# ScalarE's squares, tangents and projection casts: which instruction the weight work is issued behind

## The chip, the cores and the metric

The kernel runs on one core of a Trainium2 chip. The metric is the device time of one execution in microseconds; lower is better. The engines are called by the names the profile gives them: PE (TensorE), ACT (ScalarE), DVE (VectorE), POOL (GpSimd) and SP (SyncE, which only issues transfers here).

## What is computed

A block of 2048 tokens and 512 features goes through a layer norm, then through two branches: attention with 32 heads of 16 features over a sliding window of 256 tokens, and a gated feed-forward of width 1792. The second branch gates the first.

```python
xn = _layernorm(x, axis=-1)
s = _A_ref(xn, A_wqkv, A_wo)              # sliding-window attention
g = _silu(_B_ref(xn, B_w1, B_w3, B_w2))   # (silu(xn @ w1) * (xn @ w3)) @ w2
return x + s * g
```

## The kernel before, in words

All products are made in float16 with a high and a low half of each operand (three matmuls for one product: high by high, high by low, low by high). So each weight is prepared on the chip before its first use, and kept in DRAM for later use. The preparation of a weight tile has these steps, in this order:

- a square with a sum over the row: on ACT (`L249`, tile `sqa`, with the sums `ssq`) or, for some tiles, on DVE; for the down projection's weight w2 it is `L931`
- a cast of the sums to bf16 on DVE (`L261`, or `L935` for w2; tile `sb`)
- a small sum over all rows on PE (`L285`, `s<-sb,onesb`), placed in spare columns of an attention scores bank, beside the matmuls of a maxima row (`L667`)
- a power of two from this sum on DVE (`L294`, `L295`, `L298`, `L302`, `L304`, and for w2 `L946` to `L956`)
- the scaling on ACT (`L342`), the high half on ACT (`L343`), the low half on POOL (`L345`); for some tiles both on ACT and DVE (`L333`, `L334`)

The tokens are done in four tiles of 512 (t = 0 to 3). In each tile, the attention goes over 4 groups of heads (g) and 2 pairs in each (p). A first pass makes the scores on PE (`L667`, tiles `s` and `po`) and their maxima on DVE (`L681`); a second pass makes them again with the maximum in a row of the operand (`L748`), adds a mask on DVE (`L755`), takes the exponential on ACT (`L758`, tile `pt`) and multiplies by the values on PE (`L776`, tile `po`). Beside these batches stand dense pieces: q and k projections (PE `L597`, upper half cast by ACT `L614`, lower half by DVE `L618`), the values (`L567`, `L570`), gate and up products of the feed-forward (PE `L1048`; ACT's tanh of the gate `L1063`, DVE's `L1067`, and `L1072` for the product with up; then the halves by ACT `L1081` and POOL `L339`), and the down products (`L1273`, later `L1191` in a folded form with seven products, whose weights are sums made at t = 1 by ACT `L1003`, POOL `L1005` to `L1019` and ACT `L1015`). In tiles t > 0 the layer norm's scale comes from POOL (`L465` to `L474`, tile `rs`), and DVE applies it (`L477`).

What sets the order: PE's instructions stand in the order in which the program writes them. The other engines' queues are put in order by a scheduler, each engine then working strictly down its list. Two things bind the scheduler. `urgent()` raises the priority of an instruction. `tc.issue_after(ins)` puts what it encloses behind the instruction `ins` in the queue; the helper `behind_exp()` uses the instruction held in `lasts["exp"]`. Before the change that is the last attention exponential. It binds scalings of later gate and up weights (`tied`), squares and scalings of w2, the fold's sums, and the tanh of the output gate. `lasts["emptied"]` holds DVE's last instruction that empties a bank.

`later(n, f)` runs `f` n program steps later. `squares(..., apart=1)`, which `measure(f, 1)` calls for the gate and up weights of two blocks of 128 columns, spreads the four squares of such a pair over four steps. `f` counts these blocks, 14 in all. The squares of the pairs f = 6, 8, 10 and 12 run beside the first attention units.

The names in the code blocks and rows: `slot_N` is the N-th tile made in the general memory of 54 slots, `m` a PSUM bank of a dense piece, `s` and `po` PSUM tiles of the attention. Line numbers are those of the kernel before; in the kernel after, all lines from 253 on are 3 higher.

Of the kernel before, what the change touches and what calls it, by code (L numbers as in the profile page):

```python
# [14 lines left out]
AF = mybir.ActivationFunctionType  # L15
# [68 lines left out]
def tile_block(ctx: ExitStack, tc: tile.TileContext, x, wqkv, wo, w1, w3, w2, out):  # L84
    nc = tc.nc
# [58 lines left out]
    def later(n, f):  # L144
        made_so_far[0] += 1
        queue.append((now[0] + n, made_so_far[0], f))
# [33 lines left out]
    behind = []  # L180
# [59 lines left out]
    def squares(parts, on_act=0, apart=0):  # L240


        ssq = small.tile([P, len(parts)], F32, name="ssq")

        def one(i, raw):

            sq = ppool.tile([P, D], BF16, name="sqa" if i < on_act else "junk", bufs=1)
            if i < on_act:
                nc.scalar.activation(sq, raw, AF.Square, accum_out=ssq[:, i:i + 1])  # L249
            else:  # L250
                nc.vector.tensor_tensor_reduce(out=sq, in0=raw, in1=raw, scale=1.0, scalar=0.0,
                                               op0=ALU.mult, op1=ALU.add, accum_out=ssq[:, i:i + 1])
        for i, raw in enumerate(parts):
            if apart:
                later(apart * (i + 1), lambda i=i, raw=raw: one(i, raw))
            else:
                one(i, raw)
        sb = small.tile([P, len(parts)], BF16, name="sb")

        def cast():  # L260
            lasts["cast"] = nc.vector.tensor_copy(sb, ssq)  # L261
        def behind_bank():

            with tc.issue_after(lasts["emptied"].ins) if "emptied" in lasts else nullcontext():
                cast()
        if apart:
            later(apart * len(parts) + 2, behind_bank)
        else:
            cast()
        return sb  # L270
# [151 lines left out]
    lasts = {}  # L422
# [158 lines left out]
    def project(t, g, k, terms=(range(3),), scores_bank=False):  # L581


        cell = {}

        parts = ([[(c, i) for c in (2 * half, 2 * half + 1) for i in range(3)] for half in range(2)] if len(terms) == 1
                 else [[(c, i) for i in group for c in range(NC)] for group in terms])

        def part(n):
            assert turned[t] == 4  # L590
            w = WQ[t, g, k]
            xh, xl = X[t]
            if n == 0:
                cell["pp"] = bank([P, TW]) if scores_bank is False else scores_bank()[:, 0, :]
            for c, i in parts[n]:
                a, b = ((0, xh), (1, xh), (0, xl))[i]
                nc.tensor.matmul(cell["pp"], w[:, (a * NC + c) * P:(a * NC + c + 1) * P], b[:, c, :], start=(c, i) == parts[0][0],  # L597
                                 stop=(c, i) == parts[-1][-1])
            if n < len(parts) - 1:
                return  # L600
            if t == 0:
                def store():
                    with behind_load():
                        nc.sync.dma_start(dWQ[g, k], w)
                    give(w, after=8)
                later(45, store)
            else:
                give(w)
            pp = cell["pp"]
            both = take(F16)  # L610
            B = both.rearrange("p (a t) -> p a t", a=2)
            s = QS / (XS * WS)
            with urgent():
                nc.scalar.activation(B[:, 0, :], pp, AF.Copy, scale=s)  # L614

            def rest():
                with urgent():
                    lasts["emptied"] = nc.vector.scalar_tensor_tensor(B[:, 1, :], pp, s, B[:, 0, :], op0=ALU.mult, op1=ALU.subtract)  # L618
                d = (dQ, dK)[k][g][:, :, t * TW:(t + 1) * TW]
                if k == 0:  # L620
                    nc.sync.dma_start(d[:, 0:2, :], B[:, 0:1, :].to_broadcast([P, 2, TW]))
                    nc.sync.dma_start(d[:, 2, :], B[:, 1, :])
                else:
                    nc.sync.dma_start(d[:, 0:2, :], B)
                    nc.sync.dma_start(d[:, 2, :], B[:, 0, :])
                give(both, after=4)
            later(1, rest)
        return opening([(len(l), lambda n=n: part(n)) for n, l in enumerate(parts)])
# [408 lines left out]
    def gate_up(t, f):  # L1037
        cell = {}

        def part(k, half):  # L1040
            assert turned[t] == 4
            xh, xl = X[t]
            w = WF[t, f][0][k]
            if half == 0:
                cell[k] = bank([P, TW])
            for c in (2 * half, 2 * half + 1):
                for i, (a, b) in enumerate(((0, xh), (1, xh), (0, xl))):
                    nc.tensor.matmul(cell[k], w[:, (a * NC + c) * P:(a * NC + c + 1) * P], b[:, c, :], start=c == 0 and i == 0,  # L1048
                                     stop=c == NC - 1 and i == 2)
            if half == 0:  # L1050
                return
            if t == 0:
                def store():
                    nc.sync.dma_start(dW1[f, k], w)
                    give(w, after=4)
                later(2, store)
            else:
                give(w)
            if k == 0:
                cell["s"] = sg = take(F32)  # L1060

                with urgent():
                    nc.scalar.activation(sg, cell[0], AF.Tanh, scale=sg_scale[:, f:f + 1])  # L1063

                def product():
                    with urgent():
                        lasts["emptied"] = nc.vector.scalar_tensor_tensor(sg, sg, 1.0, cell[0], op0=ALU.add, op1=ALU.mult)  # L1067
                later(1, product)
            else:
                sg = cell["s"]  # L1070
                with urgent():
                    lasts["emptied"] = nc.vector.scalar_tensor_tensor(sg, cell[1], 0.5 * HS / (WS * XS)**2, sg,  # L1072
                                                                      op0=ALU.mult, op1=ALU.mult)
                if t > 1:
                    HH[t, f] = sg
                    later(1, lambda: (fold_second if f % 2 else fold_first)(t, f // 2))
                    return
                HH[t, f] = hh = take(F16)

                def rest():  # L1080
                    nc.scalar.copy(hh[:, 0:TW], sg)  # L1081
                    halves(nc.gpsimd.tensor_sub, hh[:, TW:], sg, hh[:, 0:TW])
                    give(sg, after=8 if t == 0 else 20)
                later(1, rest)
        return [q for k in range(2) for q in opening([(6, lambda k=k, half=half: part(k, half)) for half in range(2)])]
# [604 lines left out]
```

## Time and profile before

| what | value |
|---|---|
| median of 3 runs | 808.35 us (808.19 to 809.09) |
| profiled execution, its own time | 808.19 us |
| its span in the profile | 806.4 us |
| PE busy | 792.3 us (98%) |
| DVE, ACT, POOL busy | 630.9, 392.5, 377.5 us |
| squares on ACT by L249 | 34, median 629 ns, from 6.7 to 146.0 us |
| squares on ACT by L931 | 14, median 621 ns, from 43.8 to 191.4 us |

How to read the views: a timeline row has the start in us, the length in us, the engine, the source line, the operation, output and inputs, the shape, and in brackets how long the engine stood idle before it and what ended that. The name in the bracket is inferred; where the engine named had long been done, it was another. Rows marked x2 and more are merged. A row of the windows view has the window, its length, then busy time and count of PE, of PE's weight loads, of DVE, ACT and POOL, the granted PE clock, the DMA share and GB/s.

### The profile page before, as it was taken

How to read it: one execution, taken by the hardware profiler on the slowest of the kernel's cores; microseconds unless marked ns; L12 is line 12 of the kernel's file. 1: busy time of each engine (PE TensorE's matmuls, PEld its weight loads, DVE VectorE, ACT ScalarE, POOL GpSimd, SP SyncE). 2: the span in 40 equal slices, each digit the busy share in tenths (PEclk: the TensorE clock that was granted, in tenths of full speed). 3: DMA queues.
4: the chain of work that ended last, by engine and by line, in shares of the span. 5: the costliest groups of instructions: out<-in, count | busy, mean ns of one | idle time of the engine just before them, and what ended most of it. 6: DMA issues, size and time to landing. Idle time of an engine off the chain costs nothing.

```text
span 806.4 us, 23975 instructions
## 1 busy us (share of the span) xinstructions
PE 792.3 (98%) x9175; PEld 403.6 (50%) x9175; DVE 630.9 (78%) x2037; ACT 392.5 (49%) x591; POOL 377.5 (47%) x732
## 2 busy tenths in 40 slices
PE   8999999999999999999999999999999999999997
PEld 4444444444544444444445444466544754466465
DVE  8888888798898778887888888777768886875537
ACT  6878686663456535345443443434444234344411
POOL 2345357352439345355352555430346276650670
PEclk9999999999999999999999999999999999999999
DMA  9887554746666574658456733656462654334431
GB/s 282 241 259 241 176 177 121 260 121 196 189 194 197 151 241 129 220 150 268 118 180 177 216 110 94 187 150 186 133 169 84 160 135 132 87 89 158 129 93 59
DMA packets 109859, 134.19 MB, mean 166 GB/s; under 512 B 18928, under 2 KB 64944, under 8 KB 109744
## 3 DMA queue, kind: packets, MB, share of 16 engines
q1 hardware_dynamic: 109456, 132.13, 55.9%
q8 instruction: 72, 1.18, 0.6%
q10 hardware_dynamic: 288, 0.52, 0.2%
q14 instruction: 43, 0.35, 0.1%
HBM read 91.23 MB, written 36.57 MB: 158 GB/s over the span
## 4 chain that ended last, share of the span: by engine, by line
PE 83%; DVE 6%; ACT 6%; DMA 2%; issue 2%; SPq 1%; POOL 0%; DVEq 0%; ACTq 0%
PE m L1048 30%; PE po L776 9%; PE m L1273 9%; PE m L597 8%; PE m L1191 8%; PE s L748 5%; PE m L1325 4%; PE m L567 4%; PE s L667 3%; PE po L667 2%; ACT pt L758 1%; DVE junk L681 1%; ACT slot L342 1%; DMA slot<-in_B_w_dram 1%; ACT slot L343 1%
## 5 line engine op out<-in xcount | busy, mean ns | idle before, releaser
L1048 PE MATMUL m<-XH,slot 128*128 128x512 f16 x896 | 267.3, 380 | 1.3 <-DVE slot L618 0.8
L758 ACT ACTIVATE pt<-s,es 128x1024 f32<-128x1024 f32 x152 | 167.6, 1113 | 190.9 <-DVE s L755 179.2
L1048 PEld LDWEIGHTS <-slot 128*128 128x128 f16 x1344 | 124.9, 98 | 155.2 <-issue 11.5
L1048 PE MATMUL m<-XL,slot 128*128 128x512 f16 x448 | 169.8, 379 | 0.0
L755 DVE TENSOR_TENSOR s<-s,MK 128x256 f32<-128x256 f32 (+2 forms) x280 | 118.8, 435 | 51.9 <-PE s L748 48.9
L681 DVE CUSTOM_DVE_ANT_0 junk<-s,MW 128x320 bf16<-128x320 f32 x276 | 134.1, 486 | 17.6 <-PE s L667 9.8
L339 POOL TENSOR_TENSOR slot<-slot,slot 128x256 f16<-128x256 f32 (+1 forms) x86 | 57.6, 692 | 126.8 <-ACT slot L1081 56.7
L345 POOL TENSOR_TENSOR slot<-slot,slot 128x128 f16<-128x128 f32 x168 | 68.8, 445 | 69.7 <-ACT slot L343 67.7
L681 DVE CUSTOM_DVE_ANT_0 junk<-po,MW 128x320 bf16<-128x320 f32 x172 | 83.5, 485 | 4.7 <-DVE al L298 0.4
L1273 PE MATMUL m<-slot,slot 128*128 128x512 f16 x336 | 78.6, 380 | 0.1
L776 PE MATMUL po<-pt,V 64*32 64x320 f32 (+4 forms) x2880 | 77.2, 342 | 1.5 <-DVE pp L304 1.5
L597 PE MATMUL m<-XH,slot 128*128 128x512 f16 x240 | 70.9, 380 | 1.1 <-DVE slot L1067 0.7
L1191 PE MATMUL m<-slot,slot 128*128 128x256 f16 x588 | 68.4, 273 | 0.0
L1106 POOL TENSOR_TENSOR slot<-slot,slot 128x256 f16<-128x256 f32 x98 | 64.6, 672 | 1.1
L1063 ACT ACTIVATE slot<-m,sgs 128x512 f32<-128x512 f32 x56 | 38.3, 683 | 54.0 <-PE m L1048 53.8
L776 PEld LDWEIGHTS po<-pt,V 64*32 64x32 f32 x2880 | 50.4, 106 | 23.6 <-issue 2.4
L1191 PEld LDWEIGHTS <-slot 128*128 128x128 f16 x588 | 56.2, 98 | 11.4 <-issue 2.8
L1067 DVE SCALAR_TENSOR_TENSOR slot<-slot,m 128x512 f32<-128x512 f32 x56 | 38.3, 685 | 28.6 <-ACT slot L1063 27.1
L748 PE MATMUL s<-qa,KA 50*64 50x320 f16 (+3 forms) x1472 | 58.3, 259 | 0.2 <-DVE M L681 0.2
L597 PEld LDWEIGHTS <-slot 128*128 128x128 f16 x384 | 35.6, 98 | 44.6 <-issue 3.1
L748 PEld LDWEIGHTS <-KA 50*64 50x64 f16 x1472 | 30.1, 105 | 52.0 <-issue 31.4
L1273 PEld LDWEIGHTS <-slot 128*128 128x128 f16 x336 | 30.7, 98 | 38.4 <-issue 4.0
(190 smaller groups left out, 1138.8 us busy)
## 6 DMA issues: line engine op xcount, KB each, us to landing
slot<-dW SPq DMA_DIRECT2D x98, 256.0 KB
slot<-in_B_w_dram SPq DMA_DIRECT2D x56, 256.0 KB
slot<-dFold SPq DMA_DIRECT2D x48, 256.0 KB
dW<-slot SPq DMA_DIRECT2D x42, 256.0 KB
slot<-in_A_x_dram SPq DMA_DIRECT2D x30, 256.0 KB
KA<-dK SPq DMA_DIRECT2D x24, 288.0 KB
slot<-dWQ SPq DMA_DIRECT2D x24, 256.0 KB
qa<-dQ SPq DMA_DIRECT2D x30, 192.0 KB
```

The lines of the kernel that those rows point to most:

```text
L339: op(out[:, c], a[:, c], b[:, c])
L345: nc.gpsimd.tensor_sub(lo[:, c:c + P], raw[:, c:c + P], hi[:, c:c + P])
L597: nc.tensor.matmul(cell["pp"], w[:, (a * NC + c) * P:(a * NC + c + 1) * P], b[:, c, :], start=(c, i) == parts[0][0], stop=(c, i) == parts[ ...
L681: lasts["maximum"] = nc.vector.tensor_tensor_reduce(out=junk[:, :n], in0=s[:, r, :n], in1=mask, scale=1.0, scalar=NEG, op0=ALU.add, op1=AL ...
L748: nc.tensor.matmul(s[64 * h:64 * h + 64, r, o:o + 64 * n], ka[rows, 2 * p + a, 64 * (m + 4):64 * (m + 5)], qa[rows, 2 * p + a, 64 * (m + k ...
L755: nc.vector.tensor_add(v, v, MK[:, kind, of:of + n, :].unsqueeze(1).to_broadcast([P, 2 * len(which), n, 64]))
L758: lasts["exp"] = nc.scalar.activation(pt, s, AF.Exp, scale=es)
L776: nc.tensor.matmul(cell["po"][32 * i:32 * i + 32, h, 64 * (m + k):64 * (m + k + n)], V[64 * h:64 * h + 64, (4 * t + m // 2) % VB, hd * VW: ...
L1048: nc.tensor.matmul(cell[k], w[:, (a * NC + c) * P:(a * NC + c + 1) * P], b[:, c, :], start=c == 0 and i == 0, stop=c == NC - 1 and i == 2)
L1106: nc.gpsimd.tensor_sub(lo, view, hi)
L1191: nc.tensor.matmul(cell["ps"][:, c], made[:, f:f + P], wj[:, g:g + 256], start=j == j0 and c == 0 and n == 0, stop=j == j1 - 1 and n == 2, ...
L1273: nc.tensor.matmul(ps, hh[:, a * TW + b * P:a * TW + (b + 1) * P], w[:, c * D:(c + 1) * D], start=f == f0 and i == 0, stop=f == f1 - 1 and ...
```

## The change

Three places are edited. `lasts["exp"]` is now also set by the cast of a projection's upper half (`L614`) and by the gate's tanh (`L1063`), so that everything issued with `behind_exp()` stands behind whichever of the three came last in the program. And the squares that are spread over steps (`apart`) and run on ACT are issued with `behind_exp()` too, once a bank has been emptied.

```diff
+        def behind(i, raw):
+            with behind_exp() if i < on_act and "emptied" in lasts else nullcontext():
+                one(i, raw)
         for i, raw in enumerate(parts):
             if apart:
-                later(apart * (i + 1), lambda i=i, raw=raw: one(i, raw))
+                later(apart * (i + 1), lambda i=i, raw=raw: behind(i, raw))
             else:
                 one(i, raw)
...
             with urgent():
-                nc.scalar.activation(B[:, 0, :], pp, AF.Copy, scale=s)
+                lasts["exp"] = nc.scalar.activation(B[:, 0, :], pp, AF.Copy, scale=s)
...
                 with urgent():
-                    nc.scalar.activation(sg, cell[0], AF.Tanh, scale=sg_scale[:, f:f + 1])
+                    lasts["exp"] = nc.scalar.activation(sg, cell[0], AF.Tanh, scale=sg_scale[:, f:f + 1])
```

No instruction is added or removed. PE's list of rows is the same in both kernels. ACT's list differs from row 90 to 177 of its 499 and from 229 to 255; DVE's in three places; POOL's and SP's where rows trade places.

The first place is DVE's queue between the first attention units of tile 0. Here `sb` with `ssq` of four sums is the cast for the pair f = 8; `slot_1721` is the k projection of the last head group, `slot_1652` a gate of the feed-forward. Before:

```order
L681 ISA junk,M<-po,MW 128x320
L681 ISA M 128x1
L261 CAST sb<-ssq 128x4
L681 ISA junk,M<-po,MW 128x320
L681 ISA M 128x1
L438 BN_STATS st<-slot_1522 128x6
L618 SCALAR_TENSOR_TENSOR slot_1721<-m_1666,slot_1721 128x512
L439 BN_AGGR mv<-st 128x2
L438 BN_STATS st<-slot_1524 128x6
L1072 SCALAR_TENSOR_TENSOR slot_1652<-m_1727,slot_1652 128x512
L755 TENSOR_TENSOR s<-s,MK 128x4x64
```

and now:

```order
L684 ISA M 128x1
L441 BN_STATS st<-slot_1522 128x6
L621 SCALAR_TENSOR_TENSOR slot_1721<-m_1666,slot_1721 128x512
L442 BN_AGGR mv<-st 128x2
L441 BN_STATS st<-slot_1524 128x6
L1075 SCALAR_TENSOR_TENSOR slot_1652<-m_1727,slot_1652 128x512
L758 TENSOR_TENSOR s<-s,MK 128x4x64
L442 BN_AGGR mv<-st 128x2
L264 CAST sb<-ssq 128x4
L758 TENSOR_TENSOR s<-s,MK 128x2x64
```

The cast has moved behind the second maximum of `po`, the bn rows, L1072 (now L1075) and the first mask addition.

The second place is ACT's queue from there on. `slot_1565` and `slot_1569` are gate weights of f = 10 and 11, `slot_1829` and `slot_2003` gates of the feed-forward. Before:

```order
L249 ACTIVATE sqa,ssq<-slot_1565 128x512
L1063 ACTIVATE slot_1829<-m_1807,sgs 128x512
L342 ACTIVATE slot_1098<-slot_1098,pi 128x512
L249 ACTIVATE sqa,ssq<-slot_1569 128x512
L343 CAST slot_1831<-slot_1098 128x512
L1081 CAST slot_1915<-slot_1829 128x512
L758 ACTIVATE pt<-s,es_400 128x1024
L342 ACTIVATE slot_1099<-slot_1099,pi 128x512
L931 ACTIVATE sqa,ssq_1987<-slot_1745 128x512
L1063 ACTIVATE slot_2003<-m_1978,sgs 128x512
```

and now:

```order
L1066 ACTIVATE slot_1829<-m_1807,sgs 128x512
L345 ACTIVATE slot_1098<-slot_1098,pi 128x512
L346 CAST slot_1831<-slot_1098 128x512
L1084 CAST slot_1915<-slot_1829 128x512
L761 ACTIVATE pt<-s,es_400 128x1024
L345 ACTIVATE slot_1099<-slot_1099,pi 128x512
L249 ACTIVATE sqa,ssq<-slot_1565 128x512
L1066 ACTIVATE slot_2003<-m_1978,sgs 128x512
L346 CAST slot_1955<-slot_1099 128x512
L249 ACTIVATE sqa,ssq<-slot_1569 128x512
```

The two squares have moved behind the exponential, one ahead of the next tanh and one behind it. The same stretch ends with the tanh of `slot_2203`, ahead of which stood, and now no longer stand, two scalings (`slot_1575` of w2, `slot_1103` of f = 9). Before:

```order
L614 ACTIVATE slot_2176<-m_2100 128x512
L343 CAST slot_2082<-slot_1253 128x512
L1081 CAST slot_2080<-slot_2003 128x512
L342 ACTIVATE slot_1575<-slot_1575,sw_1974 128x512
L342 ACTIVATE slot_1103<-slot_1103,pi 128x512
L1063 ACTIVATE slot_2203<-m_2190,sgs 128x512
```

and now:

```order
L617 ACTIVATE slot_2176<-m_2100 128x512
L346 CAST slot_2066<-slot_1102 128x512
L345 ACTIVATE slot_1253<-slot_1253,sw_1974 128x512
L1084 CAST slot_2080<-slot_2003 128x512
L346 CAST slot_2082<-slot_1253 128x512
L1066 ACTIVATE slot_2203<-m_2190,sgs 128x512
L345 ACTIVATE slot_1575<-slot_1575,sw_1974 128x512
L345 ACTIVATE slot_1103<-slot_1103,pi 128x512
```

The tanh now stands directly behind the casts of `slot_2080` and `slot_2082`.

The third place is ACT's queue some 20 us later, where the last of three sums of w2 (`slot_2188`) is made for the cast `L935` with a shape of 128x3, whose sum on PE is the 64x3 one. Before:

```order
L758 ACTIVATE pt<-s,es_400 128x1024
L342 ACTIVATE slot_1570<-slot_1570,pi 128x512
L931 ACTIVATE sqa,ssq_1987<-slot_2188 128x512
L343 CAST slot_2599<-slot_1570 128x512
L249 ACTIVATE sqa,ssq<-slot_2093 128x512
L1063 ACTIVATE slot_2629<-m_2608,sgs 128x512
```

and now:

```order
L761 ACTIVATE pt<-s,es_400 128x1024
L345 ACTIVATE slot_1570<-slot_1570,pi 128x512
L249 ACTIVATE sqa,ssq<-slot_2092 128x512
L346 CAST slot_2599<-slot_1570 128x512
L249 ACTIVATE sqa,ssq<-slot_2096 128x512
L1066 ACTIVATE slot_2629<-m_2608,sgs 128x512
L934 ACTIVATE sqa,ssq_1987<-slot_2188 128x512
```

The square of `slot_2188` has moved behind two squares of the pair f = 12 and the tanh of `slot_2629`; on DVE its cast has moved behind that gate's first product (`L1067`).

## The prediction

> **What bounds the kernel now.** The page was read first: the busy shares and the chain that ended last.
>
> ```profile
> PE 792.3 (98%) x9175; PEld 403.6 (50%) x9175; DVE 630.9 (78%) x2037; ACT 392.5 (49%) x591; POOL 377.5 (47%) x732
> ...
> PE 83%; DVE 6%; ACT 6%; DMA 2%; issue 2%; SPq 1%; POOL 0%; DVEq 0%; ACTq 0%
> ```
>
> TensorE (PE) is the bound. PE's queue is the same list of rows in both kernels, so an edit to the other engines can only change the time for which PE stands still. The busy times by stage say where it does:
>
> ```profile
> 72.00:165.00 93.00, 87.53 (x1034) 42.52 (x1032) 76.71 (x292) 64.32 (x119) 46.15 (x110) 1.00 0.64 197
> 165.00:780.00 615.00, 614.10 (x7536) 314.06 (x7535) 476.03 (x1482) 266.18 (x352) 292.99 (x522) 1.00 0.54 156
> ```
>
> From 72 to 165 us PE is idle for 93.00 - 87.53 = 5.5 us; in the 615 us behind it for 0.9 us. All rows that move on ScalarE (ACT) up to row 177 lie in the first stage, and those from row 229 (weight sums of the fold) in the second, where there is next to nothing to win and where an advance or delay of PE from the first stage is simply kept. So the sum is made between 72 and 165 us, from PE's timeline there (start, length, what, and in brackets the idle time before it):
>
> ```profile
> 96.91 0.18 PE L285 MATMUL s<-sb,onesb 64*64 64x4 bf16 x4
> ...
> 97.45 0.59 PE L1048 MATMUL m<-XH,slot 128*128 128x512 f16 x2 [0.20 <-DVE slot L618]
> 97.88 0.38 PE L1048 MATMUL m<-XL,slot 128*128 128x512 f16 x1
> ...
> 112.60 0.59 PE L597 MATMUL m<-XH,slot 128*128 128x512 f16 x2 [0.73 <-DVE slot L1067]
> ...
> 115.14 0.30 PE L667 MATMUL s<-KA,qa 48*64 48x256 f16 x4 [0.74 <-ACT pt L758]
> ...
> 121.17 0.33 PE L667 MATMUL po<-KA,qa 48*64 48x320 f16 x4 [0.64 <-DVE XL L525]
> ...
> 127.70 2.04 PE L776 MATMUL po<-pt,V 64*32 64x320 f32 x72 [1.49 <-DVE pp L304]
> ...
> 136.48 4.06 PE L1273 MATMUL m<-slot,slot 128*128 128x512 f16 x18
> ...
> 145.91 0.18 PE L285 MATMUL s<-sb,onesb 64*64 64x3 bf16 x4
> ...
> 161.96 0.59 PE L597 MATMUL m<-XH,slot 128*128 128x512 f16 x2 [0.38 <-DVE slot L618]
> ...
> 163.92 0.30 PE L667 MATMUL s<-KA,qa 48*64 48x256 f16 x4 [0.15 <-ACT pt L758]
> ```
>
> Four pauses between 112 and 128 us hold 0.73 + 0.74 + 0.64 + 1.49 = 3.6 us; two at 162 to 164 hold 0.5 us. Who holds PE there is read from the timelines of VectorE (DVE) and ACT:
>
> ```profile
> 95.22 0.27 DVE L261 CAST sb<-ssq 128x4 bf16<-128x4 f32 x1
> ...
> 96.70 0.69 DVE L618 SCALAR_TENSOR_TENSOR slot<-m,slot 128x512 f16<-128x512 f32 x1 [0.21 <-ACT slot L614]
> ...
> 97.98 0.67 DVE L1072 SCALAR_TENSOR_TENSOR slot<-m,slot 128x512 f32<-128x512 f32 x1
> 98.57 0.42 DVE L755 TENSOR_TENSOR s<-s,MK 128x256 f32<-128x256 f32 x1
> ...
> 104.86 0.63 DVE L477 TENSOR_SCALAR slot<-slot,mv,rs 128x512 f32<-128x512 f32 x1 [0.38 <-POOL rs L474]
> ...
> 111.86 0.69 DVE L1067 SCALAR_TENSOR_TENSOR slot<-slot,m 128x512 f32<-128x512 f32 x1
> ...
> 115.73 0.17 DVE L261 CAST sb<-ssq 128x4 bf16<-128x4 f32 x1 [0.72 <-ACT sqa L249]
> ...
> 120.09 0.69 DVE L618 SCALAR_TENSOR_TENSOR slot<-m,slot 128x512 f16<-128x512 f32 x1 [0.90 <-ACT slot L614]
> ...
> 122.93 0.69 DVE L1067 SCALAR_TENSOR_TENSOR slot<-slot,m 128x512 f32<-128x512 f32 x1 [0.71 <-ACT slot L1063]
> ...
> 127.15 0.41 DVE L525 TENSOR_TENSOR XL<-po,XH 128x256 f16<-128x256 f32 x1
> ...
> 144.54 0.16 DVE L935 CAST sb<-ssq 128x3 bf16<-128x3 f32 x1
> ...
> 146.17 0.69 DVE L1067 SCALAR_TENSOR_TENSOR slot<-slot,m 128x512 f32<-128x512 f32 x1 [1.09 <-ACT slot L1063]
> ...
> 153.40 0.69 DVE L1067 SCALAR_TENSOR_TENSOR slot<-slot,m 128x512 f32<-128x512 f32 x1 [1.36 <-DMA slot<-dWQ]
> ```
>
> ```profile
> 96.08 0.59 ACT L614 ACTIVATE slot<-m 128x512 f16<-128x512 f32 x1
> 98.69 0.62 ACT L1081 CAST slot<-slot 128x512 f16<-128x512 f32 x1 [2.01 <-DVE slot L1072]
> ...
> 101.45 0.63 ACT L249 ACTIVATE sqa<-slot 128x512 bf16<-128x512 f32 x1
> ...
> 103.26 0.62 ACT L249 ACTIVATE sqa<-slot 128x512 bf16<-128x512 f32 x1
> ...
> 107.94 0.62 ACT L1081 CAST slot<-slot 128x512 f16<-128x512 f32 x1 [3.47 <-DVE slot L1072]
> 108.92 1.11 ACT L758 ACTIVATE pt<-s,es 128x1024 f32<-128x1024 f32 x1 [0.35 <-DVE s L755]
> ...
> 120.97 0.73 ACT L342 ACTIVATE slot<-slot,sw 128x512 f32<-128x512 f32 x1
> 121.60 0.72 ACT L342 ACTIVATE slot<-slot,pi 128x512 f32<-128x512 f32 x1
> 122.21 0.68 ACT L1063 ACTIVATE slot<-m,sgs 128x512 f32<-128x512 f32 x1
> ...
> 143.72 0.62 ACT L931 ACTIVATE sqa<-slot 128x512 bf16<-128x512 f32 x1
> ...
> 145.47 0.67 ACT L1063 ACTIVATE slot<-m,sgs 128x512 f32<-128x512 f32 x1
> ...
> 152.70 0.67 ACT L1063 ACTIVATE slot<-m,sgs 128x512 f32<-128x512 f32 x1
> ```
>
> ACT works without a gap from 108.92 us until past the tanh of 122.21. The L1067 at 122.93 waits for that tanh, and behind it DVE runs through to the L525 that ends at 127.56 and frees the bank that PE's values at 127.70 write (the page names an `L304`, but that is another tile; L525 is the one that reads `po`). The pauses at 112.60, 115.14 and 121.17 hang on the same run of ACT. So up to 127.70 the time is set by when this run of ACT and DVE begins and how long it is, not by when PE arrives, as long as PE is not over 3.6 us later.
>
> **The change part by part.** (a) *The cast at 95.22 us moves behind the L755 of 98.57.* Its squares go behind the projection's upper half (L614) into the 2.01 us that ACT idled before 98.69: free on ACT. But the cast now stands behind L618, two bn_stats, L1072 and the first L755. These rows keep their inputs, and less the cast they come some 0.1 us sooner: the cast ends near 99.05 us. PE's L285 at 96.91, a sum that reads `sb`, waits in order for that cast; so does all behind it, the L1048 of 97.45 first. L285 starts near 99.1 and L1048 0.3 us later (97.45 - 96.91 without the pause of 0.20), at 99.4: PE is 1.9 us late. Bounds: 1.4 (the cast's 0.27 and the 0.21 of idle time at 96.70 both go from DVE's path) and 2.3 (neither goes).
>
> (b) *How much of the 1.9 is left at 127.70.* What the run of ACT and DVE takes from PE in between has room: L477 at 104.86 waited for GpSimd's `rs` (0.38), L1081 at 107.94 for DVE. The chain to `rs` starts on DVE behind two maxima that now wait for L285, and I put that at 0.3 us. PE's own pauses of 0.73 + 0.74 + 0.64 + 1.49 take up the rest: 1.9 - 0.3 = 1.6 us of the 3.6 go. Bounds of what is left: 0, and 1.9 if the run shifts with PE.
>
> The length shown for one matmul, 0.38 us at 97.88, exceeds the step from one to the next, (97.88 - 97.45) / 2 = 0.215, so a pause is some 0.16 us longer than its bracket. The page "Perfetto Trace Analysis" of the Trainium skill, in its section on the lifecycle of a Tensor Engine instruction, says that a matmul's end is estimated and not observed; the trace agrees. By brackets the four pauses hold 3.6 us, by steps 3.6 + 4 x 0.16 = 4.2; either holds the 1.9.
>
> (c) *ACT's run from 108.92 to the tanh of 122.21.* Two squares that filled the idle time before 107.94 (101.45 and 103.26, 0.63 + 0.62 = 1.25 us) come into it. Two weight scalings (L342, at 120.97 and 121.60) leave it, behind the tanh: 122.21 - 120.97 = 1.24. Net 0. An exponential in the middle stands behind an L931 (0.62) in place of a shorter cast. I take +0.1 us; bounds -1.2 and +1.2 (only one of the two counts). The other cast, 115.73 us, moves behind both L755 and one maximum; it waits there for a square that ends near 117.6, so DVE's second maximum is 0.8 us later, but the 0.90 us that DVE idled for L614 before 120.09 takes that up. 0; bound +0.8.
>
> (d) *The cast at 144.54.* Its last input, L931 at 143.72, now stands behind two squares and the tanh of 145.47: tanh 145.5 to 146.0, L931 to 146.8. The cast stands behind the L1067 of 146.17 and ends near 147.0. L285 at 145.91 needs it: PE 1.1 us late, with no pause behind it until 161.96. Bounds 0.9 and 1.4.
>
> (e) *The pauses at 161.96 and 163.92* are set by ACT's L614 and an exponential, which hang on a run of DVE behind the L1067 of 153.40. That one waited 1.36 us for a tanh (the row names a load, but the tanh of 152.70 ended at 153.37); that tanh now stands ahead of two weight scalings and comes sooner, so this run does not shift with PE. PE comes later and finds them done: 0.38 + 0.15 + 2 x 0.16 = 0.85 us back. Bounds 0 and 0.85.
>
> (f) *The rest.* Ahead of 80 us two exponentials come sooner, but PE waits there for maxima on DVE, whose rows stay. In the fold's stage the weight sums go behind a tanh, and GpSimd's block of work starts later; the cover is that PE reads the halves made there well after the block, and it idles 0.9 us in all of the 615 us. On SP's queue single loads trade places with the gather or with the maxima's rows next to them. 0 for these; bounds -0.2, the 0.20 us before 97.45, and +0.5, one more pause like the shortest of the four.
>
> Sum: 1.9 - 1.6 + 0.1 + 1.1 - 0.85 + 0 = +0.65 us. The profiled execution took 808.19 us for a span of 806.4 us, and the median of the runs, 808.35 us, is 0.16 above it: 808.35 + 0.65 = 809.0 us. Those runs spread over 0.9 us (0.1%); 0.2%, or 1.6 us, is about what a measurement of this kernel can tell from no change.
>
> **The rivals.**
> *Not taken up (slower).* The 1.9 us of (a) pass to ACT's and DVE's run because L1072 at 107.2 or the maxima before it wait for PE. It decides once the run begins over 1.3 us later. Then 1.9 + 0.1 + 1.1 - 0.85 = +2.3, without (e) +3.1: 810.6 to 811.4. For it: DVE's rows there depend on PE one by one. Against it: the 3.47 us that ACT idled before 107.94. Chance 0.17.
> *A longer run of ACT (slower).* The two squares count and the two scalings do not, because the tanh of 122.21 waits for something else: +1.2 at 127.70, so 810.1. Chance 0.08.
> *A pause that slows PE's clock (slower).* PE's granted clock is 1.00 in both stages, and the 18 matmuls at 136.48 take 4.06 us, 0.22 each, though PE stood for 1.49 us 9 us before. A pause of over 2 us is not shown in this stage. If the 18 after it ran at half pace: +3.9 us, some of it taken up as in (b): 810 to 812.8. "TensorE: Matmul & The Clock Gate" of the Trainium skill, Part 1, has such a gate, at one idle window of about 3.4 us; by that rule 1.9 us is too short, and no run here shows it. Chance 0.02.
> *All waits gone (faster).* The exponentials and the tanh come sooner throughout, the two sums cost nothing, and the 3.6 + 0.5 us of pauses go: 808.35 - 4.1 = 804.2; half of it 806.3. For it: urgent work on ACT does stand earlier in the rows. Against it: the two casts stand later in DVE's. Chance 0.07.
>
> **How the numbers follow.** The forecast, +0.65 within -0.5 and +1.5, has the other 0.66. It lies within 0.2%. Slower: 0.17 + 0.07 (of 0.08) + 0.02 = 0.26. Faster by over 0.2%: 0.06 of the 0.07. Same: 0.68. The range reaches from 807.9 (the forecast with a run of (c) 1.1 us shorter) to 810.7, the near end of the first rival; outside lie most of that rival, the clock and the faster case, under 2 in 10 with what the near end holds.
>
> **What would show it.** Right: PE's L285 near 97 us starts at about 99 with a pause of some 2 us on a cast; the pauses between 112 and 128 shrink from 3.6 to about 2; a new pause of 1 us at the 64x3 sum; none at 162. Wrong: L1081 near 108 comes more than 1 us later (not taken up), the tanh near 122 moves by over 1 us against that L1081, or L285 does not wait at all.

## The result: 0.5% slower, and the profile after

The changed kernel takes 812.35 us (median of 6 runs, 812.00 to 813.86) against 808.37 us (6 runs of the kernel before): ratio 1.0051, 95% interval 1.0041 to 1.0061. The forecast was 809.0 us, with a range up to 810.7. A second set gave 811.54 us (9 runs, 809.32 to 814.10) against 808.70: ratio 1.0037, 1.0022 to 1.0053. The profiled execution took 812.11 us for a span of 810.3 us, 3.92 us more than that of before. All line numbers from 253 on are 3 higher than before (L285 is L288 now, L298 is L301, L525 is L528, L776 is L779).

TensorE's timeline (start, length, what, idle time before it in brackets), of the pauses:

```profile
99.13 0.20 PE L288 MATMUL s<-sb,onesb 64*64 64x4 bf16 x4 [1.95 <-DVE sb L264]
...
115.41 0.30 PE L670 MATMUL s<-KA,qa 48*64 48x256 f16 x4 [0.30 <-ACT pt L761]
...
121.43 0.33 PE L670 MATMUL po<-KA,qa 48*64 48x320 f16 x4 [0.63 <-DVE XL L528]
...
129.47 3.48 PE L779 MATMUL po<-pt,V 64*32 64x320 f32 x72 [3.00 <-DVE pp L307]
132.89 1.47 PE L1276 MATMUL m<-slot,slot 128*128 128x512 f16 x6
...
150.21 0.20 PE L288 MATMUL s<-sb,onesb 64*64 64x3 bf16 x4 [0.92 <-DVE sb L938]
```

Against before, TensorE is 2.22 us late at the sums (99.13 against 96.91), 1.97 at the L1051 behind them (99.42 against 97.45, where the pause of 0.20 is gone), 0.26 at 121.43, but 1.77 at 129.47 and 3.21 at 132.89 (129.68 before): the 72 matmuls took 3.48 us in place of 2.04. At 150.21 it is 4.30 late. The windows (busy time and instructions of PE, PEld, DVE, ACT, POOL, then the granted clock, the DMA share and GB/s) show the same by stage, and the clock at the values:

```profile
72.00:165.00 93.00, 84.97 (x1003) 41.15 (x1002) 75.53 (x280) 61.91 (x115) 43.12 (x103) 0.98 0.62 194
165.00:780.00 615.00, 613.52 (x7538) 312.88 (x7537) 477.39 (x1490) 268.21 (x355) 294.57 (x528) 1.00 0.54 156
...
126.00:129.40 3.40, 0.48 (x20) 0.34 (x20) 3.40 (x8) 1.32 (x4) 2.38 (x7) 0.97 0.38 106
129.40:132.80 3.40, 3.33 (x72) 1.92 (x72) 1.97 (x10) 1.49 (x3) 3.08 (x7) 0.52 0.31 96
132.80:136.20 3.40, 3.40 (x46) 1.65 (x43) 3.12 (x8) 0.00 (x0) 3.10 (x6) 1.00 0.03 7
```

For 3.4 us behind the pause the granted clock is a half; before it was 1.00 all through. What the 3.00 us wait for is seen on VectorE's and GpSimd's timeline of the changed kernel:

```profile
126.02 0.42 DVE L527 CAST XH<-po 128x256 f16<-128x256 f32 x1
126.36 2.04 DVE L301 TENSOR_SCALAR al<-al 128x4 int32<-128x4 int32 x1
128.32 0.68 DVE L1075 SCALAR_TENSOR_TENSOR slot<-m,slot 128x512 f32<-128x512 f32 x1
128.92 0.41 DVE L528 TENSOR_TENSOR XL<-po,XH 128x256 f16<-128x256 f32 x1
...
119.30 3.20 POOL L348 TENSOR_TENSOR slot<-slot,slot 128x128 f16<-128x128 f32 x8 [1.78 <-ACT slot L346]
122.45 1.30 POOL L342 TENSOR_TENSOR slot<-slot,slot 128x256 f16<-128x256 f32 x2
123.72 4.66 POOL L348 TENSOR_TENSOR slot<-slot,slot 128x128 f16<-128x128 f32 x12
129.72 1.30 POOL L342 TENSOR_TENSOR slot<-slot,slot 128x256 f16<-128x256 f32 x2 [1.35 <-DMA rb<-de]
```

and of the kernel before:

```profile
126.19 0.45 DVE L298 TENSOR_SCALAR al<-al 128x4 int32<-128x4 int32 x1
...
127.48 0.15 DVE L302 TENSOR_SCALAR pi<-al 128x4 int32<-128x4 int32 x1
127.55 0.16 DVE L304 TENSOR_SCALAR pp<-al 128x4 f32<-128x4 f32 x1
...
117.51 4.71 POOL L345 TENSOR_TENSOR slot<-slot,slot 128x128 f16<-128x128 f32 x12 [1.77 <-DMA qa<-mt]
122.18 1.30 POOL L339 TENSOR_TENSOR slot<-slot,slot 128x256 f16<-128x256 f32 x2
123.48 3.13 POOL L345 TENSOR_TENSOR slot<-slot,slot 128x128 f16<-128x128 f32 x8
```

L301 works on 128x4 numbers. It takes 2.04 us, and ends at 128.40 as GpSimd's unbroken run ends at 128.38; before, L298 ended at 126.64 and the run at 126.61. L302 and L304, of the same size, began when the run had ended, and took 0.15 and 0.16 us. L528, two rows behind L301 on VectorE, frees the bank that the values write.

GpSimd's run has not grown: in both kernels it is 22 instructions without a gap, 9.1 us in all. The two rows L339 (now L342) stand four instructions earlier in it, so that the part behind them has twelve instructions in place of eight; the texts below call this part the run of twelve, or of eight. What has changed is when the run takes place. It begins at 119.30 in place of 117.51, behind a cast of ScalarE (L346) that begins at 118.61 in place of 116.82 and has two squares (L249 at 115.77 and 117.00) in the 3 us ahead of it. So the run ends 1.77 us later, while L301 begins only 0.17 us later. The difference of 1.60 us is what L301 has grown by (2.04 - 0.45 = 1.59).

### The profile page after: what moved, and what is told of

It reads as the page before. It is cut to its first block, busy times and chain, and to the rows that moved or that the text cites. A ratio compares the mean times of both kernels' runs of the same rounds, so it can differ in the third digit from the quotient of the medians.

```text
span 810.3 us, 23971 instructions
## 1 busy us (share of the span) xinstructions
PE 794.1 (98%) x9175; PEld 404.0 (50%) x9175; DVE 632.7 (78%) x2037; ACT 392.3 (48%) x591; POOL 377.1 (47%) x732
## 4 chain that ended last, share of the span: by engine, by line
PE 82%; DVE 6%; ACT 5%; DMA 3%; issue 2%; SPq 1%; POOL 0%; ACTq 0%; DVEq 0%
PE m L1051 30%; PE po L779 9%; PE m L600 8%; PE m L1276 8%; PE m L1194 8%; PE s L751 5%; PE m L570 4%; PE m L1328 4%; PE s L670 3%; DMA slot<-in_B_w_dram 2%; PE po L670 2%; DVE junk L684 1%; ACT slot L345 1%; ACT pt L761 1%; ACT sqa L249 1%
## 5 line engine op out<-in xcount | busy, mean ns | idle before, releaser
L1051 PE MATMUL m<-XH,slot 128*128 128x512 f16 x896 | 267.3, 380 | 1.0 <-DVE slot L621 0.6
L1051 PEld LDWEIGHTS <-slot 128*128 128x128 f16 x1344 | 124.9, 98 | 155.0 <-issue 11.5
L1051 PE MATMUL m<-XL,slot 128*128 128x512 f16 x448 | 169.8, 379 | 0.0
L342 POOL TENSOR_TENSOR slot<-slot,slot 128x256 f16<-128x256 f32 (+1 forms) x86 | 57.6, 691 | 123.5 <-ACT slot L1084 60.7
L779 PE MATMUL po<-pt,V 64*32 64x320 f32 (+4 forms) x2880 | 78.7, 347 | 3.0 <-DVE pp L307 3.0
L779 PEld LDWEIGHTS po<-pt,V 64*32 64x32 f32 x2880 | 50.9, 107 | 26.1 <-issue 5.1
L1070 DVE SCALAR_TENSOR_TENSOR slot<-slot,m 128x512 f32<-128x512 f32 x56 | 38.3, 684 | 27.5 <-ACT slot L1066 27.4
```

Source lines behind the costliest of these rows:

```text
L342: op(out[:, c], a[:, c], b[:, c])
L779: nc.tensor.matmul(cell["po"][32 * i:32 * i + 32, h, 64 * (m + k):64 * (m + k + n)], V[64 * h:64 * h + 64, (4 * t + m // 2) % VB, hd * VW: ...
```

## The experiments

**Theory and rivals.** *Port theory*: L301 stands still for GpSimd's run and holds up L528; the pause that this makes costs the clock. The Trainium skill, in its page "SBUF — State Buffer", section "Who interferes with whom", has a port pair of SBUF that the two engines share under an exclusive lock, held for one instruction, for which a tensor_scalar of VectorE can contend. The rows above go further: L301 stood for some four to five GpSimd instructions of 0.39 us (4.66 / 12). *Arrival theory*: the run of ScalarE and VectorE is late as a whole. Each kernel below was timed beside the kernel before.

**1. L301 out of the way.** The edit to the changed kernel:

```
             with tc.issue_after(lasts["emptied"].ins) if "emptied" in lasts else nullcontext(), \
+                 tc.issue_after(lasts["turned"].ins) if "turned" in lasts else nullcontext():
                 chain()
...
-                    nc.vector.tensor_sub(lo, pt, hi)
+                    lasts["turned"] = nc.vector.tensor_sub(lo, pt, hi)
```

> The changed kernel with one thing more: the chain of small steps that begins with L301 is issued behind the subtraction that makes a turned block's lower half (L528). On VectorE that moves one row alone, L301, behind L1075 and L528; the orders of TensorE, ScalarE and GpSimd stay as in the changed kernel. Port theory (VectorE's 128x4 L301 stands still until GpSimd's unbroken run of twelve ends, and holds back L528, which frees the bank): L528 ends near 127.5 us, TensorE's values start at 127.5 to 127.7 in place of 129.47, the pause is 1.1 to 1.3 us in place of 3.00, the clock stays at 1.00 and the 72 matmuls take 2.04 us in place of 3.48; time 812.35 - 1.9 - 1.4 = 809.0 us. Arrival theory (ScalarE's and VectorE's run as a whole comes too late, and L301 only shows where the wait is booked): values still past 129 us, time 812.3. If the clock falls for a reason other than the long pause: 810.5.

Measured: 810.71 us (6 runs, 809.87 to 811.75), ratio 1.0028 (1.0017 to 1.0040). Its timeline (VectorE, TensorE, GpSimd):

```profile
128.40 0.41 DVE L529 TENSOR_TENSOR XL<-po,XH 128x256 f16<-128x256 f32 x1
128.73 2.40 DVE L301 TENSOR_SCALAR al<-al 128x4 int32<-128x4 int32 x1
...
128.96 2.04 PE L780 MATMUL po<-pt,V 64*32 64x320 f32 x72 [1.04 <-DVE XL L529]
...
133.46 0.25 PE L671 MATMUL s<-KA,qa 48*64 48x128 f16 x4 [0.71 <-DVE XL L529]
...
125.16 4.68 POOL L349 TENSOR_TENSOR slot<-slot,slot 128x128 f16<-128x128 f32 x12
129.79 1.31 POOL L343 TENSOR_TENSOR slot<-slot,slot 128x256 f16<-128x256 f32 x2
```

The pause ahead of the values is 1.04 us and their clock full, as the port theory has it, and the arrival theory falls. L301 itself stands even longer, again to the end of GpSimd's run (131.10), and part of the wait moves on to 133.46 (0.71). The time is not the 809.0 us of the port theory: from 103 us on all is some 1.4 us later than in the changed kernel's profile, because here the clock fell behind the first pause. The granted clock is 0.50 from 99.8 to 103.0 us. Three of the six runs have a mean clock of 0.998 (811.1 to 811.8), three 1.000 (809.9 to 810.3).

**2. Another form of the instruction.** In the changed kernel, with a small constant tile `c23` of the number 23, set at the start:

```
-            nc.vector.tensor_scalar(al.bitcast(I32), al.bitcast(I32), 24, 23, op0=ALU.logical_shift_right,
-                                    op1=ALU.logical_shift_left)
+            nc.vector.scalar_tensor_tensor(al.bitcast(I32), al.bitcast(I32), 24, c23[:, 0:n],
+                                           op0=ALU.logical_shift_right, op1=ALU.logical_shift_left)
```

> The changed kernel with L301 (and all its like) written as a scalar_tensor_tensor against a small constant tile of 23 in place of a tensor_scalar with two numbers; same result, same place in every engine's order (one memset of 128x8 more at the start). Port theory, in the form that only some forms of VectorE's instructions stand still while GpSimd runs: the L301 at 126.36 takes 0.15 to 0.2 us in place of 2.04, values start near 127.6, the clock stays at 1.00; time 809.0 us. If every instruction with all its data in SBUF stands still, or if L301 waits for its input or a semaphore: 2 us as before, 812.3 us.

Measured: 810.08 us (12 runs, 808.38 to 814.65), ratio 1.0024 (1.0010 to 1.0039). Its timeline:

```profile
127.04 2.04 DVE L303 SCALAR_TENSOR_TENSOR al<-al,c 128x4 int32<-128x4 int32 x1
...
124.40 4.66 POOL L350 TENSOR_TENSOR slot<-slot,slot 128x128 f16<-128x128 f32 x12
```

This form stands to the end of the run too, so the expectation of 0.2 us failed. The same section of the skill counts a VectorE instruction with two inputs in SBUF among those that contend, and this form has two: by that rule it could not have escaped, and the trace agrees. What was not foreseen is the spread: six runs lie between 808.4 and 809.8 us, at a clock of 0.999 or 1.000, and six between 810.3 and 814.7 at 0.995 to 0.998. One and the same program loses time in some executions and not in others.

**3. The pause filled.** In the changed kernel, 12 matmuls of ones just ahead of the values:

```
+                if (t, g, p) == (0, 1, 0):
+                    fill = scores_bank()[:, 0, :].rearrange("p (k q) -> p k q", q=P)
+                    for _ in range(12):
+                        nc.tensor.matmul(fill, onesb, onesb.unsqueeze(1).to_broadcast([P, 4, P]), start=True, stop=True)
+                    scores_bank()
```

> The changed kernel with 12 matmuls of ones (128x512) into a spare bank of scores just ahead of the values that wait: their result is not used, they only keep TensorE at work for some 2.6 of the 3.0 us of the pause. Clock theory (the granted clock falls because TensorE stands still for 3.0 us): the values start at 129.5 as before, or up to 0.3 later, but take 2.04 us in place of 3.48; time 812.35 - 1.4 = 810.9 us. If the clock falls for another reason (the kind of matmul, heat, the time in the program): 3.4 us as before, 812.3 to 812.6 us. Port and arrival theory say the same here, since what ends the wait is untouched.

Measured: 810.32 us (7 runs, 809.70 to 811.90), ratio 1.0023 (1.0013 to 1.0034). Its timeline:

```profile
126.43 2.76 PE L771 MATMUL s<-onesb 128*128 128x512 bf16 x12
129.12 2.05 PE L784 MATMUL po<-pt,V 64*32 64x320 f32 x72
...
126.38 0.51 DVE L301 TENSOR_SCALAR al<-al 128x4 int32<-128x4 int32 x1
...
123.73 4.67 POOL L348 TENSOR_TENSOR slot<-slot,slot 128x128 f16<-128x128 f32 x12
```

The clock stays up, and six of seven runs are at 1.000. But this profile does not separate the theories of the clock, since L301 took 0.51 us here, with the same run of twelve at the same place: it ended at 126.89, near the end of the run's eighth instruction (123.73 + 8 x 0.39 = 126.85). So L301's length, too, differs from execution to execution. In this profile GpSimd works on without a gap behind the run, and VectorE's next four small rows are long as well: 0.31, 0.47, 0.60 and 0.71 us, where in the changed kernel, with GpSimd idle, they took 0.15 to 0.17. The same four lengths stand in the profile of experiment 4. So it is not L301 alone that waits.

**4. A longer run in the kernel before.**

```
-        for c in range(0, 512, P):
-            nc.gpsimd.tensor_sub(lo[:, c:c + P], raw[:, c:c + P], hi[:, c:c + P])
+        for _ in range(1 + again):
+            for c in range(0, 512, P):
+                nc.gpsimd.tensor_sub(lo[:, c:c + P], raw[:, c:c + P], hi[:, c:c + P])
```

with `again` 1 for the last of the four halves that the run ends with.

> The kernel before, in which GpSimd makes the last four subtractions of its run at 123.48 twice (the second time writes the same values): its unbroken run gets four instructions, some 1.55 us, longer and ends near 128.2 in place of 126.61; every other engine's order stays as before. Port theory: L298 at 126.19 stretches from 0.45 to about 2.0 us, TensorE's pause ahead of the values grows from 1.49 to about 3.0 us; the clock falls as in the changed kernel, and the 72 matmuls take 3.4 us; time 808.37 + 1.55 + 1.4 = 811.3 us, or down to 810.5 if the pauses near 162 us take up what they can; 809.9 if the clock does not fall. Rival (GpSimd's length is of no matter to VectorE there): 808.4 us, L298 0.45 us.

Measured: 808.79 us (11 runs, 808.08 to 809.73), ratio 1.0005 (0.9997 to 1.0014). Its timeline:

```profile
126.39 0.44 DVE L298 TENSOR_SCALAR al<-al 128x4 int32<-128x4 int32 x1
...
123.69 4.66 POOL L346 TENSOR_TENSOR slot<-slot,slot 128x128 f16<-128x128 f32 x12
```

A miss: L298 was let in after 0.44 us, though GpSimd's run went on, and none of the 11 runs is above 809.73 us. By the port theory a wait of 2 us needs a run that goes on for as long; this shows that such a run is not enough. What else decides is not shown.

**5. The changed kernel again, and 6. both pauses filled.** The second is experiment 3 with 14 matmuls more, ahead of the sums of 99 us. A draw is from here on what differs between executions of one program: whether L301 waits long, and whether the clock falls behind a pause.

> The changed kernel itself once more, beside the other runs of this set, so that their times have it on the same chip. The theory now: two things are drawn anew in each execution. VectorE's L301 is let in at the next end of a GpSimd instruction (0.5 us) or only at the end of its run (2.0 us); and TensorE's clock, after a pause of 1.95 or 3.0 us, is halved for 3.4 us or not. By that the times spread from 809.5 us (neither) to 814 us (both pauses, and L301 late), with clocks of 0.995 to 1.000, and the median lies at 811 to 812.5. Rival: each run the same, 812.0 to 813.9 as in the first six.

> The kernel with 12 filling matmuls ahead of the values near 127 us, and 14 more (128x128 of ones, into unused columns of the bank of scores) ahead of the sums near 97 us that wait 1.95 us for the cast: both long pauses of TensorE are filled, nothing waits less. Clock theory (a pause of 1.95 us is enough in some executions): clock 1.000 in every run, spread at most 1.2 us, median 809.9 to 810.2 us, a little under the 810.3 of the run with one pause filled, whose highest (811.9 us at 0.998) no longer occurs. Rival (clock falls for other reasons): still runs at 0.998 or below, and times up to 812.

Measured: the changed kernel as said above; its nine runs lie at 809.3 to 809.6 (three, clock 1.000), 811.5 to 812.2 (three, 0.997 to 0.999) and 813.9 to 814.1 (three, 0.995 to 0.996). With both pauses filled 810.47 us (8 runs, 809.79 to 812.30), ratio 1.0025 (1.0015 to 1.0035); seven of the eight runs at 0.999 or 1.000, one at 0.997, for which no profile was kept. The profile of the changed kernel, and behind it that of the filled one:

```profile
126.80 2.08 DVE L301 TENSOR_SCALAR al<-al 128x4 int32<-128x4 int32 x1
...
129.95 2.04 PE L779 MATMUL po<-pt,V 64*32 64x320 f32 x72 [3.02 <-DVE pp L307]
```

```profile
126.42 2.07 DVE L303 TENSOR_SCALAR al<-al 128x4 int32<-128x4 int32 x1
...
129.55 2.04 PE L786 MATMUL po<-pt,V 64*32 64x320 f32 x72 [0.32 <-DVE pp L309]
```

The first pair shows a pause of 3.02 us behind which the clock did not fall: a pause of this length is not enough for the loss. The second shows L301 held for 2.07 us and TensorE kept at work: of the loss only the wait is left. The 14 matmuls do not fill the first pause whole; 1.06 us of it stay. Seven of eight runs at 0.999 or more, against four of the changed kernel's 15, support that idle time of TensorE is what costs the clock. The expectation of a full clock in every run failed, so other causes of a fall are not ruled out. The rival of equal runs falls.

**7. Without the squares, and 8. the squares alone.** Line `behind(i, raw)` put back to `one(i, raw)`; or `lasts["exp"] =` taken away at the tangent and the projection.

> The changed kernel without its part on the squares: they are issued as before, while ScalarE's weight work still follows the tangent and the projection's upper half. Theory (the squares' delay of the two casts is what makes TensorE wait): the sums near 97 us wait 0.2 us, not 1.95; the 64x3 sums near 146 us do not wait; time 808.4 to 809.3 us, clock 0.999 or more. Rival (the tangent's and projection's bindings lengthen GpSimd's run and cost as much): a long L301 or a pause of over 2 us at the values near 128 us stays, 810.5 us or more.

> The kernel before with the squares' part of the change alone. Theory: the 1.95 us pause at the sums near 97 us and the 0.9 us at the 64x3 sums near 146 us are there, with half of the runs losing 1.5 us of clock; time 809.5 to 811 us. What it lacks of the changed kernel's 812.35 is then what GpSimd's merged run of twelve (from the tangent's binding) adds at 128 us. Rival (the cost needs both parts, one alone costs nothing): 808.4 us.

Measured: without the squares 807.65 us (11 runs, 807.26 to 809.06), ratio 0.9989 (0.9980 to 0.9997), under the kernel before and under the 808.4 to 809.3 us expected. Its profile is of its slowest run (809.06 us, clock 0.997), and shows a third place where the clock can fall, near the start of the program and behind waits of 1.26 and 0.56 us (before 8.93 and 10.35 us):

```profile
10.60:14.00 3.40, 3.40 (x17) 3.15 (x16) 2.91 (x6) 1.85 (x4) 0.00 (x0) 0.51 1.15 290
```

The kernel before waits there for 1.03 and 0.57 us, and in its profile the clock is 1.00. ScalarE's list is the same there (it differs from row 90 on), so this loss does not belong to the change. Squares alone 810.14 us (12 runs, 808.48 to 813.13), ratio 1.0021 (1.0009 to 1.0033): five runs at 808.5 to 808.9 (clock 0.999 or more), four at 810.1 to 810.2 (0.998), three at 812.0 to 813.1 (0.995 to 0.997). The steps of 1.5 us and more fit the draws; in the runs that lose none the squares alone cost nothing that can be measured. The rival for the tangent and the projection falls. GpSimd's run of twelve comes with the squares alone (4.68 us from 123.75), so the expectation that the tangent's binding makes it was wrong. In this profile L301 took 0.51 us and the values began at 127.98, 0.28 us later than in the kernel before.

**9. The tangent alone, and 10. the projection alone.** Only one of the two `lasts["exp"] =` is added to the kernel before.

> The kernel before with the tangent's part of the change alone (ScalarE's weight work waits for the last of exponential and tangent; squares and projection as before). Theory (the gain of the kernel without squares, 1.0 us, is the two pauses near 162 us, and the tangent's part brings it): 807.7 to 807.9 us, no pause at 162 and 164 us. Rival (the projection's part brings it): 808.5 us, both pauses still there.

> The kernel before with the projection's part of the change alone. Theory: only some 0.2 us near 74 us are gained, 808.4 us, and the pauses of 0.38 and 0.15 us near 162 and 164 us stay. Rival (it brings the gain): 807.7 us, no pauses there.

Measured: tangent 807.44 us (11 runs), ratio 0.9990 (0.9981 to 0.9999); projection 808.48 us (11 runs), ratio 1.0000 (0.9991 to 1.0009). TensorE's rows of the tangent's kernel near 162 us, without a bracket:

```profile
161.45 0.59 PE L600 MATMUL m<-XH,slot 128*128 128x512 f16 x2
...
163.08 0.29 PE L670 MATMUL s<-KA,qa 48*64 48x256 f16 x4
```

Both pauses are gone though TensorE came no later, and it stands 0.84 us ahead of the kernel before.

**11. L301 shifted against GpSimd.** The changed kernel with one small copy in GpSimd's run, ahead of the rows that L301 meets (in its profile it stands at 122.28; `shift` is set for one half alone):

```
+        if shift:
+            nc.gpsimd.tensor_copy(lo[:, 0:4], raw[:, 0:4])
```

> The changed kernel with one small GpSimd instruction more (a 128x4 copy of about 0.2 us, overwritten by the next) inside its run ahead of the eight that L301 meets: the later instructions of the run come 0.2 us, half an instruction, later, all else stays. L301 then arrives some 0.3 of the way through a GpSimd instruction, where it had arrived at 0.74 to 0.81 in the kernels with a lot drawn (2.0 us in four profiles, 0.5 in two) and at 0.93 to 0.97 in those let in at once (three profiles). Theory (where in the instruction it arrives decides): the runs no longer fall into two groups; either all let in, 809.5 to 811.5 us with the clock lost only at the pause of 1.95 us, or all held to the end of the run, 812 to 814 us. Rival (a lot whatever the arrival): the same spread as the changed kernel, 809.3 to 814.1 us, median 811.5.

Measured: 810.40 us (11 runs, 809.02 to 811.22), ratio 1.0019 (1.0011 to 1.0028): five runs at 1.000 (809.0 to 810.3), six at 0.998 (810.4 to 811.2), none above. Its timeline, and its windows at the first pause:

```profile
127.81 0.33 DVE L301 TENSOR_SCALAR al<-al 128x4 int32<-128x4 int32 x1
...
129.21 2.04 PE L781 MATMUL po<-pt,V 64*32 64x320 f32 x72 [1.28 <-DVE XL L530]
...
125.36 4.68 POOL L350 TENSOR_TENSOR slot<-slot,slot 128x128 f16<-128x128 f32 x12
```

```profile
96.00:99.40 3.40, 1.45 (x26) 0.57 (x23) 3.15 (x10) 2.60 (x8) 0.86 (x4) 1.00 1.03 391
99.40:102.80 3.40, 3.40 (x13) 1.19 (x10) 2.83 (x19) 1.68 (x3) 1.63 (x5) 0.51 1.02 333
102.80:106.20 3.40, 3.40 (x58) 1.68 (x60) 1.36 (x4) 1.92 (x3) 1.88 (x9) 0.99 0.92 333
```

With an instruction more on GpSimd the group at 813 to 814 us is gone (none of 11 runs; five of the changed kernel's 15). That supports the theory that where L301 meets GpSimd's instructions matters. The medians of the two kernels are of different sets and their intervals overlap, so that one is faster is not shown. In the profile what is left is one draw, at the pause of 1.95 us, behind which the clock is a half for 3.4 us. Two runs at a clock of 1.000 (810.1 and 810.3 us) lie 1 us above the other three, and why is open.

**12. The best of it.** Experiment 7 with the edit of experiment 1.

> The changed kernel without the squares' part, and with the chain that begins with L301 issued behind the lower half's subtraction L528 (on VectorE only L301 moves, behind L1075 and L528). In the kernel without the squares GpSimd idles for 1.3 us behind its run of eight, so L301 finds the way free there. Theory: pause ahead of the values 1.1 us in place of 1.5, nothing new behind it; 807.65 - 0.35 = 807.3 us, 0.15 to 0.2% under the kernel before. Rival (the wait moves on, as in the run where L301 was put behind L528 in the changed kernel and a new pause of 0.71 us came 4 us later): 807.6 us.

Measured: 807.17 us (11 runs, 806.89 to 808.07) against 808.48, ratio 0.9983 (0.9974 to 0.9991): 0.17% under the kernel before, and under all runs of the changed one. Its timeline:

```profile
127.21 0.16 DVE L301 TENSOR_SCALAR al<-al 128x4 int32<-128x4 int32 x1
...
127.44 2.04 PE L780 MATMUL po<-pt,V 64*32 64x320 f32 x72 [1.13 <-DVE al L301]
...
123.58 3.14 POOL L349 TENSOR_TENSOR slot<-slot,slot 128x128 f16<-128x128 f32 x8
127.69 1.32 POOL L343 TENSOR_TENSOR slot<-slot,slot 128x256 f16<-128x256 f32 x2 [0.98 <-ACT slot L1085]
```

L301 falls into GpSimd's idle time and takes 0.16 us; the pause is 0.36 us shorter than before.

## Why the prediction was wrong

- *(a) The cast at 95.22 us*: right. L288 at 99.13 with 1.95 us of pause, and the product behind it 1.97 us late; forecast 99.1, "some 2 us" and 1.9.
- *(b) What is left at 127.70*: right up to 121.43 us, where 0.26 us is left. The first two pauses shrank (0.73 to none that a bracket shows, 0.74 to 0.30), the third did not (0.64 and 0.63). It failed at the last of the four, which was counted on with the others and doubled instead, from 1.49 to 3.00 us.
- *(c) ScalarE's run from 108.92*: the tangent's L1070 came 0.17 us later than before (123.10 against 122.93), where +0.1 was forecast. But the step took the time up to the values to be set by that run's start and length, with VectorE's rows behind it as long as before. One, L301, grew from 0.45 to 2.04 us. This is the step that failed: it followed ScalarE and VectorE and put at nothing what GpSimd does beside them, whose run ends 1.77 us later. L298's 0.45 us for 128x4 numbers, beside 0.15 for L302 and 0.16 for L304 of the same size, stood in the profile before and was not read.
- *The clock rival* (chance 0.02) was right in kind and much too low. In the changed kernel's profile it cost 1.44 us at 129.47. The page "TensorE: Matmul & The Clock Gate" of the Trainium skill, Part 1, names one idle window of about 3.4 us, and by that rule 1.9 us was called too short. In these runs a shorter pause was enough at times: of the seven profiles with the pause of 1.95 us, two (experiments 1 and 11) have the clock at a half for 3.4 us right behind it, and experiment 7 lost it behind waits of 1.26 and 0.56 us. The measurement decides. The same part calls the window free-running, which fits a loss that comes and goes with the run; that it is the cause was not tested.
- *(d) The 64x3 sums*: right, 1.1 us (from 3.21 late to 4.30).
- *(e) The pauses at 162 and 164 us*: right in size, 0.95 us back against 0.85 (from 4.32 late to 3.37). Experiment 9 shows they go by the tangent's part alone, without TensorE being late: in the changed kernel, that gain is spent on the lateness of (a) and (d).
- *(f) The rest*: mis-sized, 0 against +0.55 (3.37 late at 173 us, 3.92 at the end), just past its bound of +0.5. Two short pauses of TensorE add 0.35 us each, of which other rows win back a little. The first, with VectorE's row that it waits for:

```profile
280.44 0.49 DVE L684 CUSTOM_DVE_ANT_0 junk<-po,MW 128x320 bf16<-128x320 f32 x1 [0.50 <-DVE M L684]
...
281.52 0.33 PE L670 MATMUL po<-KA,qa 48*64 48x320 f16 x4 [0.39 <-DVE M L684]
```

  The row shows no other engine that VectorE could have waited for. The pair of pauses (281.5 and 327.3 us) is in both profiles of the changed kernel and in those of experiments 1 and 11, and in no other. Its cause is open.

The sum without the failed step, from the profile's own terms, is 0.26 + 1.1 - 0.95 + 0.55 = +0.96 us: 808.35 + 0.96 = 809.3 us. The three runs of the changed kernel that kept a clock of 1.000 took 809.3 to 809.6 us. So the forecast is near that of a run that loses neither draw, and most runs lose one or both. How often is known from 15 runs of the changed kernel: three. That a run of 812 us or more without a profile had a long L301 is inferred from its time and clock.

## What to carry to other kernels

Read the shortest rows of an engine too: one that is three times as long as its like (0.45 us beside 0.15) may be waiting for something that no bracket shows, and what it waits for can come later. Cost a delay by the pause it makes as well as by the lateness it leaves: on this kernel a pause of TensorE of 1.5 us cost no clock in five profiles, and one of 2 or 3 us cost about another 1.5 us in four cases of ten. Where the times of one kernel fall into groups, give the forecast as a draw between them; and split a change of several parts, since here the tangent's part alone was a gain (ratio 0.9990) and the squares' part the loss.

## What the runs showed of the hardware

- A VectorE instruction on 128x4 numbers in SBUF stood still to the end of GpSimd's run (2.04 us in the changed kernel) or was let in at the end of an instruction inside it (0.51 us in experiment 3), with VectorE's and GpSimd's rows there in the same order. With GpSimd's later instructions 0.2 us later, none of 11 runs took more than 811.22 us. Which arrivals lose is open: in experiment 1 it stood 2.40 us. The wait is part of the row's length and no bracket shows it.
- In the profiles that show a loss behind a pause (1.95 us in experiments 1 and 11, 3.00 in experiment 2 and in the first of the changed kernel), the granted clock was a half for 3.4 us; behind the 3.02 us of experiment 5 it was not lost at all. In experiment 7 it was lost for as long near the start of the program, behind waits of 1.26 and 0.56 us.
